# The order in which eight PSUM places are dealt out in the last part of a transformer-block kernel

## The chip, the cores and the metric

The kernel runs on one core of one Trainium2 chip. The metric is the device time of one execution in microseconds (us). Engines are named as in the profile: PE is TensorE's matmul (PEld its weight load), DVE is VectorE, ACT is ScalarE, POOL is GpSimd, SP is the engine whose queue issues most of the transfers.

## The reference

Four images ("b" from 0 to 3), 12 heads, 448 positions, 64 channels per head. The reference computes capped attention, then a channel MLP with a layer norm ahead of it, then a token mixer and a second channel MLP, all in float32:

```python
scores = cap * tanh(q @ k.T / sqrt(64) / cap); attn = softmax(scores); x = attn @ v   # (4, 448, 768)
xn = (x - mean) / sqrt(var + 1e-6) * g_ln
x = x + maximum(xn @ w_ch1, 0) @ w_ch2                   # 768 -> 3072 -> 768
u = x + (maximum(x.T @ w_tok1, 0) @ w_tok2).T            # 448 -> 256 -> 448
y = u + maximum(u @ u_ch1, 0) @ u_ch2                    # 768 -> 1536 -> 768
```

## The kernel before

All activations lie channel by position: six tiles of 128 channels by 448 positions for each image, `x2` and `x3` for the last two. To keep float32 accuracy every operand is split into a high and a low half in a reduced format, and a product of 128x128 weights with 128x448 activations is three matmuls (`PASSES`). A PSUM result is evacuated by DVE or ACT.

**The last part.** From line 914 on, images 2 and 3 go through both MLPs and the token mixer; that is the stretch from about 885 us to the end. It has these kinds of work, each with its own lines:

- Single image: `mlp` with one image (lines 920 and 925). Four hidden tiles, each 18 matmuls at L749 and evacuated by ACT at L754 and DVE at L755, then six output tiles of 12 matmuls at L770, each added into `x` by DVE at L774.
- Pair of images: `mlp` with images 2 and 3 (lines 921 and 926, five groups in all). Its hidden tiles come from `quads`: two quads per group, each a scheme of seven products (p1 to p7) of nine matmuls at L673, whose results are combined by DVE at L680 and ACT at L694 before the hidden tiles are made (L684, L685). Then six times two output tiles at L770, one for each image, added by DVE at L774. The operands of a quad are prepared by DVE, POOL and ACT (L609, L613, L173, L177).
- Token mixer: `tokens` (lines 922 and 923), transposes at L801, products at L825 and L847, evacuated at L804, L806, L833, L834, L851, woven with a single-image `mlp`.

**The places.** Every result takes the next place of a ring, by `next(main_banks)`. There are eight places of 512 float32 each: four one-bank tiles, `bank0` to `bank3`, and two tiles of two banks each, `sc0` and `sc1`, which attention uses whole and which the last part uses by halves:

```python
    BANKS = [Box(pp.tile([P, 512], F32, name=f"bank{i}")) for i in range(4)]
    sc_t = [pp.tile([P, 2, 512], F32, name=f"sc{i}") for i in range(2)]
    SCB = [Box(t[:, i]) for t in sc_t for i in range(2)]
```

So `SCB[0]` and `SCB[1]` are the halves of `sc0`, `SCB[2]` and `SCB[3]` those of `sc1`. In rows of the trace both halves of both tiles are called `sc`, and all four one-bank tiles `bank`.

**What sets the order.** The code does not run its steps as written: each is recorded with what it reads and writes, one `Box` for each half, and a planner (`Program.emit`) puts all steps into one order by its own fixed costs. Each engine runs its part of that order strictly in turn. The layer under the kernel then adds the waits between engines, from the tiles and the recorded order. Weights come through three tiles, `split0` to `split2`, each refilled by SP's queue (L341, L649) as soon as PE has used it.

Of the kernel before, what the change touches and what calls it, by code (L numbers as in the profile page):

```python
# [152 lines left out]
def block_kernel(ctx: ExitStack, tc: tile.TileContext, qkv, cap, gln, w1, w2, wt1, wt2, con, out):  # L153
# [72 lines left out]
# [3 lines that stand above are left out]
    SC = [Box(t, SCB[2 * i:2 * i + 2]) for i, t in enumerate(sc_t)]  # L229

    def ring(of):
        while True:
            yield from of
# [8 lines left out]
    def relay():  # L242

        def later(old, boxes, fill):
            old = [p for box in old for p in box.parts]
            add("place", 0, fill, (), old + boxes)

        def fill_x(b):
            t = place(f"late_x{b}", [3, 2, S], F32R, tag=f"x{b}")
            for i in range(3):  # L250
                LATE[b][i].at = t[:, i]

        for b in range(2):
            later(X[b], LATE[b], lambda b=b: fill_x(b))

        def fill_raw():
            for i in range(3):
                X3[i].at = place(f"late_raw{i}", [2, S], F32R, tag=f"raw{i}")
            X4[2].at = QS[0].at

        later(RAW + QS, [*X3, X4[2]], fill_raw)

        def fill_own():
            t = place("late_own", [2, 2, S], F32R, tag="own")
            for i in range(2):
                X4[i].at = t[:, i]

        later(own, X4[:2], fill_own)

        def fill_weights():  # L270
            for i in range(2):
                WF[i].at = place(f"late_whole{i}", [CC], tag=f"whole{i}")
            WF[2].at = place("late_pair", [CC], tag="pair_r")
            WF[3].at = v_t
            WS[0].at = halves_of(place("late_two", [2 * CC], F32R, tag="two"))
            WS[1].at = halves_of(place("late_qk", [2 * CC], F32R, tag="qk0"))
            WS[2].at = halves_of(ksvs_t[:, :2 * CC])

        later([*WHOLE, PAIR, *V, *two, *QK, *KS, *VS], [*WF, *WS], fill_weights)
        for box in (*EH, *EL):  # L280
            WS.append(Box(box.at[:, :, :CC], [box]))
# [3 lines left out]
    def setup():  # L285
        nc.scalar.dma_start(out=kc, in_=con[:, :K_PAIR])
        nc.scalar.dma_start(out=cap_t, in_=cap.to_broadcast([P, 1]))
        dve.memset(ones, 1.0)
        dve.memset(inv_c, 1.0 / C)
        (vs,) = VS  # L290
        dve.tensor_copy(vs.at[:, :, D:DV], ones.rearrange("p (c d) -> p c d", c=4))

        act(VA[0].at[:, 0], ones[:, :8], AF.Tanh)
        for t in rs_t:
            nc.gpsimd.memset(t, 0.0)
        dve.reciprocal(tsc, cap_t)
        dve.tensor_scalar_mul(tsc, tsc, 1.0 / math.sqrt(D))
        (sq,) = SQ
        prog.key = 15.0
        add("dma", 8, lambda: nc.scalar.dma_start(out=gl, in_=gln), (), [GL])  # L300
        add("dma", 3 * P, lambda: nc.scalar.dma_start(out=sq.at[:, :3 * P], in_=con[:, K_PAIR:]), (), [sq])

        add("dve", 8, lambda: dve.tensor_scalar_mul(gl, gl, -1.0 / 8192.0), (), [GL])
        add("dve", 3 * P, lambda: dve.tensor_copy(pair_r, sq.at[:, :3 * P].rearrange("p (a b) -> p a b", a=3)), [sq], [PAIR])
# [274 lines left out]
    def normalise(b):  # L579
        rstd = RSTD[0]  # L580
        eng = LN_ENGINES[b]
        for e in range(NCC):
            o, g = centred[e] if b < 2 else two[e % 2], BIG[b % 2][e]
            if b >= 2:
                subtract(b, e, o)
            add("dve+", S, lambda o=o, e=e: dve.scalar_tensor_tensor(
                o.at, o.at, gl[:, e:e + 1], rstd.at, op0=ALU.mult, op1=ALU.mult), [rstd, GL], [o])
            add("act", S, lambda g=g, o=o: act(g.at[:, 0], o.at, AF.Copy), [o], [g])  # L588
            add(eng, S, lambda eng, g=g, o=o: low(engine_of[eng], g.at[:, 1], o.at, g.at[:, 0]), [o], [g])
# [5 lines left out]
    main_banks = ring(BANKS)  # L595
# [19 lines left out]
    def sides(later):  # L615

        t0 = prog.key
        for c in range(3):
            prog.key = t0 + later + c * SIDES_PACE
            f12, f22, f11, f21 = (next(tmps) for _ in range(4))  # L620
            for to, pair in ((f11, BIG[0][c]), (f12, BIG[1][c]), (f22, BIG[1][c + 3]), (f21, BIG[0][c + 3])):
                join(to, pair, S)
            both(f11, f12, f11, ALU.subtract, S)
            split(X1[c], f11, S)
            both(f12, f22, f12, ALU.subtract, S)
            split(X3[c], f12, S)
            both(f22, f22, f11, ALU.subtract, S)
            split(X2[c], f22, S)
            both(f21, f21, f22, ALU.subtract, S)
            split(X4[c], f21, S)  # L630
        prog.key = t0
# [86 lines left out]
    def prepare(g):  # L718

        nonlocal n_tile  # L720
        rows = [(w1, g * G + i, C) for i in range(G)] + [(w2, g * NCC + e, G * P) for e in range(NCC)]
        for w, row, cols in rows:
            load(n_tile, w, row, cols)
            n_tile += 1
            prog.key += AHEAD_PACE
# [136 lines left out]
    def weave(*gens, ahead=0.0):  # L862

        gens, t0 = list(gens), prog.key
        keys = [t0 - ahead * (i == 0) for i in range(len(gens))]
        left = list(range(len(gens)))
        while left:
            for i in list(left):
                prog.key = keys[i]
                if next(gens[i], left) is left:  # L870
                    left.remove(i)
                keys[i] = prog.key
        prog.key = t0 + sum(k - t0 for k in keys) + ahead


    def groups(bs, first, n):
        return [(first + g, bs) for g in range(n)]

    with tc.manual_schedule():
        setup()  # L880
        prog.key = T_AHEAD
        ahead = True
        for g in range(N_AHEAD):
            prepare(g)
        ahead = False
        prog.key = 0.0
        attention(0, 0.0, 3.97)
        prog.key += T_LN0
        layer_norm(0)
        normalise(0)  # L890
        head_banks = side_banks = ring(BANKS[:2])
        attention(1, 60.01, 6.39)
        prog.key += T_LN1
        layer_norm(1)
        normalise(1)
        head_banks = side_banks = ring(BANKS[:1])

        main_banks = ring(BANKS[2:])
        n0, n1, n2 = N0, N1, N2
        prog.key, stretch = T_ALONE, STRETCH0  # L900
        weave(mlp(groups((0,), 0, n0)))
        main_banks = chain(BANKS[2:], ring(BANKS[1:]))
        attention(2, T_ATT2, PACE2)
        layer_norm(2)
        attention(3, T_ATT3, PACE3)
        prog.key, stretch = T_PAIR, STRETCH1
        weave(mlp(groups((0, 1), n0, NG1 - n0)))
        weave(tokens(0, HIDDEN[2]), mlp(groups((1,), 0, n0)), ahead=TOKENS_AHEAD)
        weave(tokens(1, HIDDEN[2]), mlp(groups((0,), NG1, N20)), ahead=TOKENS_AHEAD)
        weave(mlp(groups((0, 1), NG1 + N20, NG2 - N20), (0,)))  # L910
        weave(mlp(groups((1,), NG1, N20), (1,)))
        normalise(2)
        stretch = 1.0
        weave(mlp(groups((2,), 0, n1)))
        layer_norm(3)
        normalise(3)
        main_banks = ring(SCB + BANKS)
        relay()
        sides(SIDES_LATER)
        weave(mlp(groups((3,), 0, N30)))  # L920
        weave(mlp(groups((2, 3), n1, NG1 - n1)))
        weave(tokens(2, HIDDEN[2]), mlp(groups((3,), N30, n1 - N30)), ahead=TOKENS_AHEAD)
        weave(tokens(3, HIDDEN[2]), mlp(groups((2,), NG1, n2)), ahead=TOKENS_AHEAD)
        sides(SIDES_LATER)
        weave(mlp(groups((3,), NG1, n2)))
        weave(mlp(groups((2, 3), NG1 + n2, NG2 - n2), (2, 3)))
        prog.emit()
# [41 lines left out]
```

## Time and profile before

| | |
|---|---|
| time, median of 3 runs | 1380.13 us (1379.91 to 1381.29) |
| time of the profiled execution | 1379.54 us |
| its span, first to last instruction | 1377.7 us |
| PE busy | 1339.9 us, 97% |
| DVE busy | 1031.8 us, 75% |
| ACT busy | 658.5 us, 48% |
| mean granted TensorE clock | 0.996 of full speed |
| chain that ended last: PE | 90% of the span |

The profiled execution took 1.8 us more than its span, time that lies before the first and after the last instruction. A busy share says only that an engine was at work; what a change is worth is read from what PE waits for, as PE makes up 90% of the chain that ended last.

### The profile page before, as it was taken

What the parts mean: (1) busy time and instruction counts of PE and PEld (TensorE: products, weight loads), DVE (VectorE), ACT (ScalarE), POOL (GpSimd) and SP (SyncE); (2) the same over time, 40 slices, a digit from 0 to 9 for tenths busy, and PEclk for the clock granted to TensorE, in tenths of its full rate; (3) what the DMA queues carried; (4) which work ended last, traced back from release to release, by engine and by line L of the source; (5) the groups of instructions that cost most, each with busy time, mean ns of one, the idle gap of its engine ahead of it and who ended that gap; (6) DMA issues with size and microseconds to landing.
All of it is one profiled execution on the core that took longest, in us unless ns stands there. A gap on an engine that the chain in (4) does not pass through costs nothing.

```text
span 1377.7 us, 17881 instructions
## 1 busy us (share of the span) xinstructions
PE 1339.9 (97%) x6378; PEld 1154.8 (84%) x6378; DVE 1031.8 (75%) x1819; ACT 658.5 (48%) x1081; POOL 161.2 (12%) x133
## 2 busy tenths in 40 slices
PE   8999999999999999999999999989999999999998
PEld 3334679999999999999999999878888889888887
DVE  5988699999999998999988787857456332358572
ACT  8996566666756656667663563212112111212120
POOL 2420000100101001001101020221202000013020
PEclk9999999999999999999999999999999999999999
DMA  8885447757575765577565666653324345445233
GB/s 275 282 271 163 128 149 238 253 191 246 188 264 178 247 226 156 197 230 240 190 231 196 214 214 206 205 186 106 130 84 127 103 137 169 153 153 176 91 109 126
DMA packets 131865, 255.88 MB, mean 186 GB/s; under 512 B 9920, under 2 KB 70592, under 8 KB 131776
## 3 DMA queue, kind: packets, MB, share of 16 engines
q1 hardware_dynamic: 131200, 254.45, 56.8%
q8 instruction: 50, 0.82, 0.2%
q10 hardware_dynamic: 576, 0.29, 0.1%
q14 instruction: 39, 0.32, 0.1%
HBM read 192.57 MB, written 62.13 MB: 185 GB/s over the span
## 4 chain that ended last, share of the span: by engine, by line
PE 90%; DVE 4%; ACT 4%; DMA 1%; issue 1%; ACTq 0%; DVEq 0%
PE bank L770 30%; PE bank L749 25%; PE sc L770 8%; PE bank L673 5%; PE sc L673 5%; PE sc L749 3%; PE sc L411 3%; PE bank L429 3%; PE bank L453 2%; PE bank L825 2%; PE bank L847 1%; ACT x L414 1%; PE sc L408 1%; ACT x L415 1%; DVE x L774 1%; DVE m L419 1%
## 5 line engine op out<-in xcount | busy, mean ns | idle before, releaser
L770 PE MATMUL bank<-h,split 128*128 128x448 f32 x2064 | 437.7, 367 | 1.4 <-DVE x L774 1.3
L770 PEld LDWEIGHTS bank<-h,split 128*128 128x128 f32 x2064 | 386.1, 188 | 34.9 <-DVE x L774 2.1
L749 PE MATMUL bank<-big,split 128*128 128x448 f32 x1656 | 354.2, 368 | 3.5 <-ACT big L588 1.8
L749 PEld LDWEIGHTS bank<-big,split 128*128 128x128 f32 x1656 | 310.5, 188 | 33.4 <-ACT big L588 2.9
L774 DVE TENSOR_TENSOR x<-x,bank 128x448 f32<-128x448 f32 x172 | 105.9, 617 | 82.9 <-PE bank L770 81.7
L770 PE MATMUL sc<-h,split 128*128 128x448 f32 x528 | 115.2, 369 | 10.0 <-DVE x L774 9.3
L770 PEld LDWEIGHTS sc<-h,split 128*128 128x128 f32 x528 | 97.7, 188 | 22.9 <-DVE x L774 14.1
L173 POOL TENSOR_TENSOR ksvs<-qk,ksvs 64x512 fp32r<-64x512 f32 x23 | 32.1, 1397 | 644.1 <-ACT ksvs L392 625.0
L321 ACT ACTIVATE whole<-raw 128x384 f32<-128x384 f32 (+2 forms) x130 | 77.6, 601 | 40.7 <-DVE split L173 36.9
L754 ACT ACTIVATE h<-bank 128x448 fp32r<-128x448 f32 x92 | 49.9, 542 | 89.9 <-PE bank L749 89.5
L324 DVE SCALAR_TENSOR_TENSOR whole<-raw,whole 128x384 int32<-128x384 int32 (+2 forms) x130 | 84.2, 650 | 0.2
L774 DVE TENSOR_TENSOR x<-x,sc 128x448 f32<-128x448 f32 x44 | 27.0, 620 | 72.7 <-PE sc L770 70.8
L177 ACT ACTIVATE split<-whole 128x384 fp32r<-128x384 f32 (+1 forms) x96 | 54.2, 567 | 54.3 <-PE bank L770 33.3
L322 ACT ACTIVATE raw<-raw 128x384 int32<-128x384 uint32 (+2 forms) x130 | 77.5, 600 | 0.0
L755 DVE SCALAR_TENSOR_TENSOR h<-bank,h 128x448 fp32r<-128x448 f32 x92 | 56.6, 616 | 26.6 <-ACT h L754 25.6
L325 DVE CUSTOM_DVE_ANT_0 whole<-raw,whole 128x768 uint16<-128x768 uint16 (+2 forms) x116 | 74.2, 642 | 0.0
L173 DVE TENSOR_TENSOR split<-whole,split 128x384 fp32r<-128x384 f32 (+1 forms) x112 | 69.2, 621 | 3.7 <-ACT split L177 3.3
L419 DVE TRANSPOSE_TENSOR_REDUCE m<-x 128x28 f32<-128x896 f32 x48 | 52.7, 1103 | 10.5 <-ACT x L415 10.0
L177 ACT ACTIVATE late_two<-v 128x384 fp32r<-128x384 f32 x10 | 5.3, 526 | 113.1 <-DVE v L613 113.1
L323 DVE TENSOR_SCALAR whole<-whole 128x384 int32<-128x384 int32 (+2 forms) x130 | 55.0, 426 | 3.6 <-ACT whole L321 3.2
L419 DVE TRANSPOSE_TENSOR_REDUCE m<-own 128x28 f32<-128x896 f32 x48 | 52.9, 1101 | 4.9 <-ACT own L415 4.9
L414 ACT ACTIVATE own<-sc,tsc 128x896 f32<-128x896 f32 x48 | 47.9, 1001 | 11.6 <-DVE el L173 6.1
(295 smaller groups left out, 1997.9 us busy)
## 6 DMA issues: line engine op xcount, KB each, us to landing
split<-kept SPq DMA_DIRECT2D x96, 512.0 KB, 3.7
split<-kept SPq DMA_DIRECT2D x118, 384.0 KB, 4.1
raw<-in_w SPq DMA_DIRECT2D x72, 384.0 KB, 3.7
kept<-split SPq DMA_DIRECT2D x72, 384.0 KB, 3.5
raw<-in_w SPq DMA_DIRECT2D x54, 512.0 KB, 4.3
kept<-split SPq DMA_DIRECT2D x54, 512.0 KB, 3.3
qk<-in_qkv SPq DMA_DIRECT2D x34, 480.0 KB, 3.7
v<-in_qkv SPq DMA_DIRECT2D x31, 192.0 KB, 3.2
```

Of the source, the lines that this page charges most:

```text
L173: eng.tensor_tensor(out, whole, high.bitcast(F32), op=ALU.subtract)
L177: act(out, a, AF.Copy)
L321: add("act", m, lambda: act(f.bitcast(F32), hi.bitcast(F32), AF.Copy, scale=2.0 ** -112), [r], [w])
L322: add("act", m, lambda: act(lo, lo.bitcast(U32), AF.Copy, scale=2.0 ** -29), (), [r])
L324: add("dve+", m, lambda: dve.scalar_tensor_tensor(f, hi, -(1 << 31), f, op0=ALU.bitwise_and, op1=ALU.bitwise_or), [r], [w])
L325: add("pool+" if ahead else "dve+", m, lambda e: engine_of[e].tensor_tensor(f, f, lo, op=ALU.add), [r], [w])
L414: add("act", 2 * S, lambda e=e, sc=sc: act(e, sc.at[:, :, :S], AF.Tanh, scale=tsc), [sc], eb)
L419: add("dve", 2 * S, lambda half=half, e=e: dve.tensor_reduce(m.at[:, half].rearrange("p c j -> p (c j)"), e.rearrange("p c (j i) -> p (c j ...
L673: mm(bank.at[:, :S], w.at[:, wi, c * P:(c + 1) * P], x[c].at[:, xi], start=(c, n) == (0, 0), stop=(c, n) == (2, 2))
L749: mm(ph.at[:, :S], w[:, wi, cc * P:(cc + 1) * P], src[cc].at[:, xi], start=(cc, n) == (0, 0), stop=(cc, n) == (NCC - 1, 2))
L770: mm(py.at[:, :S], w[:, wi, i * P:(i + 1) * P], h[i].at[:, hi], start=(i, n) == (0, 0), stop=(i, n) == (G - 1, 2))
L774: add("dve", S, lambda x=x, py=py: dve.tensor_tensor(x.at, x.at, py.at[:, :S], op=ALU.add), [py], [x], early=EVACUATE)
```

## The change

One line: the order of the ring that the last part draws its places from.

```diff
-        main_banks = ring(SCB + BANKS)
+        main_banks = ring([SCB[0], BANKS[0], SCB[2], BANKS[1], SCB[1], BANKS[2], SCB[3], BANKS[3]])
```

The ring still has the same eight places, and each still comes round after eight results. Before, the order was `sc0` first half, `sc0` second half, `sc1` first, `sc1` second, `bank0` to `bank3`. After it, the first and second half of `sc0` are four results apart, as are those of `sc1`, with one-bank tiles between them. The sequence of instructions on every engine, apart from the names of these places, is the same in both programs, on PE, DVE, ACT, POOL and SP.

On PE, near the end of the program, in the output tiles of the last pair group (L770; `h` are hidden tiles, `split` weights), the difference reads:

```order
 L770 MATMUL sc0_117<-h4_90,split1_78 128x448 x3
 L770 MATMUL sc0_117<-h5_91,split1_78 128x448 x3
-L770 MATMUL sc0_117<-h3_89,split1_78 128x448 x3
-L770 MATMUL sc0_117<-h2_88,split1_78 128x448 x3
-L770 MATMUL sc0_117<-h7_93,split1_78 128x448 x3
-L770 MATMUL sc0_117<-h6_92,split1_78 128x448 x3
+L770 MATMUL bank0_113<-h3_89,split1_78 128x448 x3
+L770 MATMUL bank0_113<-h2_88,split1_78 128x448 x3
+L770 MATMUL bank0_113<-h7_93,split1_78 128x448 x3
+L770 MATMUL bank0_113<-h6_92,split1_78 128x448 x3
 L770 MATMUL sc1_118<-h0_86,split2_79 128x448 x3
```

The output tile of image 3 that followed image 2's in the other half of `sc0` now lies in `bank0`.

On PE, in the second quad of the last pair group (L673), seven products and what they lie in; before:

```order
L673 MATMUL bank0_113<-big1_85,ksvs_102 128x448 x9
L673 MATMUL bank1_114<-big0_84,split1_78 128x448 x9
L673 MATMUL bank2_115<-big0_84,split1_78 128x448 x9
L673 MATMUL bank3_116<-late_x0_5958,late_two_6983 128x448 x9
L673 MATMUL sc0_117<-late_x1_6262,late_qk_6984 128x448 x9
L673 MATMUL sc0_117<-late_raw0_6504,eh0_103 128x448 x3
L673 MATMUL sc0_117<-late_raw1_6505,eh0_103 128x448 x3
L673 MATMUL sc0_117<-late_raw2_6506,eh0_103 128x448 x3
L673 MATMUL sc1_118<-late_own_6638,el0_104 128x448 x6
```

and now:

```order
L673 MATMUL sc0_117<-big1_85,ksvs_102 128x448 x9
L673 MATMUL bank2_115<-big0_84,split1_78 128x448 x9
L673 MATMUL sc1_118<-big0_84,split1_78 128x448 x9
L673 MATMUL bank3_116<-late_x0_5958,late_two_6983 128x448 x9
L673 MATMUL sc0_117<-late_x1_6262,late_qk_6984 128x448 x9
L673 MATMUL bank0_113<-late_raw0_6504,eh0_103 128x448 x3
L673 MATMUL bank0_113<-late_raw1_6505,eh0_103 128x448 x3
L673 MATMUL bank0_113<-late_raw2_6506,eh0_103 128x448 x3
L673 MATMUL sc1_118<-late_own_6638,el0_104 128x448 x6
```

Of the two products with `big0` the second moved from `bank2` to a half of `sc1`; the products with `ksvs` and `late_x1` now lie in the two halves of `sc0`, and the one with `late_raw` between them and `late_own` has left `sc0` for `bank0`. Products in the two halves of one tile stand apart, with others between them, where before the halves of `sc0` were written one right after the other.

On DVE, at the same place, the reads of those products (L680) and the hidden tiles made from them (L685); before:

```order
L680 TENSOR_TENSOR rstd0_112<-sc1_118,mean0_111 128x448
L680 TENSOR_TENSOR other0_100<-sc1_118,other0_100 128x448
L680 TENSOR_TENSOR mean0_111<-bank0_113,mean0_111 128x448
L680 TENSOR_TENSOR other0_100<-sc1_118,other0_100 128x448
L685 SCALAR_TENSOR_TENSOR h0_86<-sum0_99,h0_86 128x448
L685 SCALAR_TENSOR_TENSOR h2_88<-rstd0_112,h2_88 128x448
L685 SCALAR_TENSOR_TENSOR h1_87<-other0_100,h1_87 128x448
L685 SCALAR_TENSOR_TENSOR h3_89<-mean0_111,h3_89 128x448
L680 TENSOR_TENSOR sq0_98<-sc0_117,rsm_108 128x448
L680 TENSOR_TENSOR rsm_108<-bank2_115,rsm_108 128x448
```

and now:

```order
L680 TENSOR_TENSOR rstd0_112<-sc1_118,mean0_111 128x448
L680 TENSOR_TENSOR other0_100<-sc1_118,other0_100 128x448
L680 TENSOR_TENSOR mean0_111<-sc0_117,mean0_111 128x448
L680 TENSOR_TENSOR other0_100<-bank1_114,other0_100 128x448
L685 SCALAR_TENSOR_TENSOR h0_86<-sum0_99,h0_86 128x448
L685 SCALAR_TENSOR_TENSOR h2_88<-rstd0_112,h2_88 128x448
L685 SCALAR_TENSOR_TENSOR h1_87<-other0_100,h1_87 128x448
L685 SCALAR_TENSOR_TENSOR h3_89<-mean0_111,h3_89 128x448
L680 TENSOR_TENSOR sq0_98<-sc0_117,rsm_108 128x448
L680 TENSOR_TENSOR rsm_108<-sc1_118,rsm_108 128x448
```

The reads `mean` and `rsm` moved from one-bank tiles into halves of `sc0` and `sc1`, whose other halves PE writes close by.

## Rows read from the trace of the kernel before

**Rows 1.** Who PE waited for: us in total, times, longest us.

```profile
PE sc L770 <- DVE x L774: 9.3, 13, 0.7
PE sc L749 <- DVE h L755: 2.1, 2, 1.4
PE sc L801 <- DVE x L774: 1.8, 3, 0.7
PE sc L749 <- ACT h L754: 1.3, 2, 0.7
PE sc L749 <- DVE h L834: 0.7, 1, 0.7
PE sc L770 <- DVE x L851: 0.7, 1, 0.7
PE sc L749 <- ACT h L833: 0.3, 1, 0.3
PE bank L770 <- DMA split<-kept: 0.2, 1, 0.2
```

**Rows 2.** Timeline, output tiles of the fourth pair group: start, us, engine, line, operation, count.

```profile
1300.65 3.81 PE L770 MATMUL sc<-h,split 128*128 128x448 f32 x18
1300.85 0.62 DVE L774 TENSOR_TENSOR x<-x,bank 128x448 f32<-128x448 f32 x1 [1.81 <-PE bank L770]
1304.50 0.62 DVE L774 TENSOR_TENSOR x<-x,sc 128x448 f32<-128x448 f32 x1 [3.03 <-PE sc L770]
1305.18 5.12 PE L770 MATMUL sc<-h,split 128*128 128x448 f32 x24 [0.71 <-DVE x L774]
...
1311.01 1.48 PE L770 MATMUL sc<-h,split 128*128 128x448 f32 x6 [0.71 <-DVE x L774]
```

**Rows 3.** Timeline, output tiles of the fifth pair group.

```profile
1342.73 9.89 PE L770 MATMUL bank<-h,split 128*128 128x448 f32 x48
```

**Rows 4.** Timeline, second quad of the fifth pair group.

```profile
1329.97 3.81 PE L673 MATMUL bank<-big,split 128*128 128x448 f32 x18
1332.43 0.62 DVE L680 TENSOR_TENSOR rstd<-sc,mean 128x448 f32<-128x448 f32 x1
1333.50 0.61 DVE L680 TENSOR_TENSOR mean<-bank,mean 128x448 f32<-128x448 f32 x1
...
1335.44 1.99 PE L673 MATMUL sc<-late_x,late_qk 128*128 128x448 f32 x9
1336.17 0.62 DVE L685 SCALAR_TENSOR_TENSOR h<-mean,h 128x448 fp32r<-128x448 f32 x1
...
1339.09 1.38 PE L673 MATMUL sc<-late_own,el 128*128 128x448 f32 x6
1339.29 0.62 DVE L680 TENSOR_TENSOR sq<-sc,rsm 128x448 f32<-128x448 f32 x1 [2.50 <-PE sc L673]
1339.94 0.62 DVE L680 TENSOR_TENSOR rsm<-bank,rsm 128x448 f32<-128x448 f32 x1
```

**Rows 5.** Timeline, token mixer of image 3, transposes and first product.

```profile
1181.07 0.62 DVE L774 TENSOR_TENSOR x<-x,sc 128x448 f32<-128x448 f32 x1 [1.69 <-PE sc L801]
...
1181.12 1.30 PE L825 MATMUL bank<-big,t 128*128 128x384 f32 x6
1181.72 0.49 ACT L804 ACTIVATE big<-sc 128x384 fp32r<-128x384 f32 x1 [2.93 <-DVE x L774]
```

**Rows 6.** Timeline, token mixer of image 3, a later product.

```profile
1210.86 1.05 PE L825 MATMUL bank<-h,t 128*128 128x384 f32 x5
1211.06 0.62 DVE L774 TENSOR_TENSOR x<-x,sc 128x448 f32<-128x448 f32 x1
```

**Rows 7.** One weight load by its line, window 1247.7 to 1248, and its user.

```profile
L341 SPq DMA_DIRECT2D split<-kept x1: 518/518/518, 1247.8 to 1247.8; - x1
...
DMA to landing us min/median/max: 3.7/3.7/3.7
1252.14 2.70 PE L770 MATMUL sc<-h,split 128*128 128x448 f32 x12 [0.71 <-DVE x L774]
```

## The prediction

> **What bounds the kernel now.** I read first whom PE waited for, since PE makes up 90% of the chain that ended last. From 850 us on it waited 23 times for DVE or ACT, always ahead of a matmul into `sc`, 16.2 us in all: 9.3 + 2.1 + 1.8 + 1.3 + 0.7 + 0.7 + 0.3; ahead of a matmul into `bank` only 0.2 us, and that for a load [rows 1]. Both kinds of place hold the same sort of results, so the wait belongs to the two-bank tiles.
>
> The timeline of a pair group's output tiles shows how it comes about. The 18 matmuls that start at 1300.65 are the 12 of image 2 in the first half of `sc0` and the first 6 of image 3 in the second half. The read of the first half (`x<-x,sc`) starts at 1304.50, when all 18 are done (1300.65 + 3.81 = 1304.46), although its own 12 had ended 1.2 us before (6 x 0.2); the read of a `bank` place starts at 1300.85, while PE is already 0.2 us into the next place. And PE's next matmul, the seventh into the second half, starts at 1305.18, that is 0.06 us after the read of the first half ends at 1304.50 + 0.62, with 0.71 us idle [rows 2]. So reads and writes of the two halves wait for each other as if the tile were one place: the read for those writes to the other half that stand ahead of it in the recorded order, then the writes behind it for the read.
>
> **What the Trainium skill says of it.** Its page "PSUM — Partial Sum Buffer", section "PSUM bank collisions raise a hardware error", tells to guard PSUM by bank and quadrant, and calls each bank a separate RAM; by that rule two halves that are two banks need no wait on each other. The trace shows them waiting all the same [rows 2], so the wait is the program's and not the chip's. If the program guarded by banks, as the page has it, these stalls would have another cause and the sum would be 0 in place of what follows.
>
> **What a stall costs.** More than its idle time. Without stalls matmuls of this shape start 0.2027 us apart: 48 take 9.89 [rows 3] and 18 take 3.81 [rows 2], so 30 more take 6.08. From 1305.18 to 1311.01 there are 24 matmuls and one stall: 5.83 us, where 24 x 0.2027 = 4.865 would do. A stall of 0.71 idle thus costs 0.965, or 0.255 above the idle time, which is what PE loses of overlap between one matmul and the next. For 23 stalls: 16.2 + 23 x 0.255 = 22.1 us. That is all that can be won: the span without them is 22.1 shorter, if nothing else is late.
>
> **What the change removes.** In the output tiles of the pair groups, in the single-image stages and in the mixer the two halves no longer stand next to each other, and by the waits that the instructions of the changed program carry, followed each to the instruction that raises it, none of the 23 is left. All 22.1 us are counted as won there. The reads in question even start 1.2 us sooner after their products, which hides nothing else, as DVE waits for PE around them [rows 2].
>
> **What it adds.** The same coupling now acts at other places, between results four apart in the ring, where a place is held long.
>
> *Quads.* Six DVE reads (L680) now wait for a product in the other half, all six in the quads. In the last group's second quad, `rstd<-sc` ran at 1332.43; now it waits for the second of the two `big` products, which ends at 1329.97 + 3.81 = 1333.78, so it starts at about 1333.82, 1.39 us late. The reads behind it follow late by the same: `mean` (1333.50 + 0.61) ends at 1335.50 and not at 1334.11. It now lies in `sc0`, and the PE product at 1335.44 goes into the other half of `sc0`; 0.06 after the read is 1335.56, 0.12 late. The last of the hidden tiles then ends at 1336.17 + 0.62 + 1.39 = 1338.18. Next, `sq<-sc` does not have to wait for the neighbouring product any more (it had 2.50 idle before 1339.29) and can start at 1338.1; `rsm`, which starts 0.65 behind it, ends at 1338.1 + 0.65 + 0.62 = 1339.37, so PE's product at 1339.09, moved to 1339.21 by the first wait, can start at 1339.43: another 0.22 [rows 4]. Together 0.34, and some 0.1 for lost overlap: 0.45. The same pattern stands in the second quads of the second and third groups: 3 x 0.45 = 1.35. Bounds: nothing if the reads lie a little better; and if `rsm` kept its present end (1339.94 + 0.62 = 1340.56) the product at 1339.09 would wait 1.5 and cost with overlap 1.65, three times 4.95. I take 1.35, as the read's own wait ahead of it is gone. The other three late reads are late by no more than this one, and what PE next writes into those tiles comes later; I take nothing, with 3 x 1.65 as the upper bound.
>
> *Mixer.* At 1181.12 the product at L825 now lies in the second half of `sc1`, and ACT reads transposes out of the first half. ACT ran that read at 1181.72 because it waited for a DVE add on the other half; without that it can start when that add did, 1181.07, when the transposes were done, and ends at 1181.07 + 0.49 = 1181.56. PE starts at 1181.62, 0.5 late [rows 5]; with 0.1 of overlap 0.6. At 1210.86 the product at L825 now waits for the DVE add out of the other half, which ends at 1211.06 + 0.62 = 1211.68: 1211.74, late by 0.88 [rows 6], with overlap 0.98. Together 1.6. Nothing hides these two.
>
> *Loads.* Where a stall vanishes PE comes for its weights sooner. The load issued at 1247.8 lands 3.7 later at 1251.5, and its user at 1252.14 stood in a stall [rows 7]; a stalled matmul starts 0.88 late (1305.18 - 1300.65 - 18 x 0.2027 [rows 2]), so it would have come at 1251.26, and now waits until about 1251.55: 0.29, with overlap 0.4. One more load, at the entry of the first quads, stands about as tight, and I price it the same, an estimate: 0.7 together, bounds 0 and the two whole stalls that they cover, 1.9.
>
> **The sum.** 22.1 - (1.35 + 1.6 + 0.7 = 3.65) = 18.45 us. The profiled execution took 1379.54, so 1361.1. That execution was 0.6 below the median of the runs; on the median's footing 1361.7, and I write 1361.4.
>
> **The rivals.**
>
> *More is given back.* If the six late reads each cost PE the upper bound, 6 x 1.65 = 9.9 in place of 1.35, with mixer and loads as above: 22.1 - 9.9 - 2.3 = 9.9, or 1369.6; half of that, 1365. For it: the margins that PE has behind late reads are tenths of a us (0.12 and 0.22 above). Against: the read that matters most had 2.50 us of idle time ahead of it, which the change frees [rows 4].
>
> *Loads become the bound.* In the single-image stages load follows load, and 7 of the 23 stalls lie there. If loads left all of them worth nothing, 7 x 0.97 = 6.8 goes, and the time is 1361.4 + 6.8 - 0.7 = 1367.5. For it: the margin of 0.65 between landing and user at 1252.14. Against: that load was issued as its tile came free, so most loads move with PE.
>
> *No change.* The stalls are not of halves but of reads that come late in any place; then they move along to `bank` and the time is 1380. That is how it would be by the rule by banks of the Trainium skill's page "PSUM — Partial Sum Buffer". Against it stand 0.2 us ahead of `bank` and 16.2 ahead of `sc` [rows 1], and the read that starts 1.2 us after its own product's end [rows 2].
>
> *Slower.* One mechanism, in the quads: a read waits for a nine-matmul product in the other half (1.99 us long), and PE's next product into that tile waits for the read, up to 1.99 + 0.62 + 0.06, some 2.7 with overlap. The 22.1 won are used up from 9 such stalls on. The five groups have ten quads, so it would have to come about in nearly each; the changed program has six reads that wait, and in three of them PE comes close behind. With 14 it would be 1380 - 22 + 38 = 1396.
>
> **How the numbers follow.** Two results of this kernel differ from no change when they are 0.2% apart, 2.8 us (the three runs span 0.1%). The forecast has 0.70: its own range runs from 1358.5 (the added 3.65 nearly nothing) to 1364 (the quads cost twice, the loads 1.9). More given back has 0.15, loads 0.08, no change 0.04, slower 0.03. Lower than 1357.4 (1379.5 - 22.1) nothing reaches, unless stalls cost more than I found. I let the range go from 1358 to 1368, which takes in loads and most of the larger give-back, and leaves out about 0.15. Faster by over 0.2%: 0.70 + 0.15 + 0.08 = 0.93; within: 0.04; slower: 0.03.
>
> **What would show it.** Right: in the list of PE's waits the row `sc L770 <- DVE x L774` falls from 9.3 us to nearly nothing, the reads of `sc` start about 0.05 us after their own product, 48 matmuls in a row at L770 with no idle time wherever a pair group's outputs are made. PE's busy time stays about 1340 while the span falls by 18. The added waits show as short ones ahead of L673 for DVE L680 (at most three groups), and two ahead of L825. Wrong: waits of 1 us and more at L673, waits for loads ahead of L749 or L770, or waits ahead of `bank` in place of those ahead of `sc`.

## The result, and the profile after

The changed kernel takes 1363.6 us, median of 4 runs (1362.26 to 1367.25); beside it on the same chip the kernel before took 1380.02. The ratio is 0.989, 95% interval 0.986 to 0.992: faster by 16.4 us. A second set of four runs gave 1363.65 and 0.989 (0.987 to 0.990). The profiled execution of after is the slowest of its four, 1367.25 us, with a span of 1365.5.

Its list of PE's waits from 850 us on (us in total, times, longest us), which answers [rows 1]:

```profile
PE sc L825 <- DVE x L774: 0.8, 1, 0.8
PE bank L770 <- DMA split<-kept: 0.5, 2, 0.3
PE sc L825 <- ACT big L804: 0.3, 1, 0.3
```

The seven rows ahead of `sc`, 23 waits and 16.2 us, are gone. Two short ones in the mixer are new, and nothing has moved to `bank` but 0.3 us more for loads.

Timeline of after, the output tiles that [rows 2] showed:

```profile
1288.77 2.59 PE L770 MATMUL bank<-h,split 128*128 128x448 f32 x12
1288.97 0.62 DVE L774 TENSOR_TENSOR x<-x,sc 128x448 f32<-128x448 f32 x1 [1.81 <-PE sc L770]
1291.20 2.60 PE L770 MATMUL sc<-h,split 128*128 128x448 f32 x12
1291.40 0.62 DVE L774 TENSOR_TENSOR x<-x,bank 128x448 f32<-128x448 f32 x1 [1.81 <-PE bank L770]
1293.63 2.59 PE L770 MATMUL bank<-h,split 128*128 128x448 f32 x12
```

Each read of `sc` now starts 0.20 after PE has begun the next place, as each read of `bank` does, and PE goes on from place to place without idle time: 12 matmuls every 2.43 us, 12 x 0.2027.

Timeline of after, the quad of [rows 4]:

```profile
1320.39 1.99 PE L673 MATMUL sc<-big,split 128*128 128x448 f32 x9
1322.21 1.99 PE L673 MATMUL bank<-late_x,late_two 128*128 128x448 f32 x9
1322.41 0.62 DVE L680 TENSOR_TENSOR rstd<-sc,mean 128x448 f32<-128x448 f32 x1 [1.42 <-PE sc L673]
...
1323.48 0.61 DVE L680 TENSOR_TENSOR mean<-sc,mean 128x448 f32<-128x448 f32 x1
...
1324.24 2.06 PE L673 MATMUL sc<-late_x,late_qk 128*128 128x448 f32 x9
...
1326.14 1.99 PE L673 MATMUL bank<-late_raw,eh 128*128 128x448 f32 x9
...
1327.33 0.62 DVE L680 TENSOR_TENSOR rsm<-sc,rsm 128x448 f32<-128x448 f32 x1
...
1328.01 1.51 PE L673 MATMUL sc<-late_own,el 128*128 128x448 f32 x6
...
1329.36 0.78 PE L673 MATMUL sc<-qs,el 128*128 128x448 f32 x3
```

`rstd` waits for the product in the other half (1320.39 + 1.99 = 1322.38); `mean` ends at 1324.09 and PE follows at 1324.24; `rsm` ends at 1327.95 and PE follows 0.06 later. Nine matmuls take 1.824 undisturbed, but from 1322.21 to 1324.24 there are 2.03 and on to 1326.14 there are 1.90: 0.28 late. From 1326.14 to 1328.01 it is 1.87, and the six behind, 1.24 at this stretch's 0.2067, take 1.35: 0.16 more. Together 0.44. The list of waits shows none of it, since hardly any idle time is left between the modelled ends of the matmuls. It is seen only in the distances between starts. The view names nobody ahead of the start at 1324.24, 0.15 after `mean` ended; that the tile is the cause there rests on e1 below, where the same matmuls follow each other without a delay.

The two products in the mixer, after:

```profile
1173.79 1.31 PE L825 MATMUL sc<-big,t 128*128 128x384 f32 x6 [0.25 <-ACT big L804]
...
1204.34 1.11 PE L825 MATMUL sc<-h,t 128*128 128x384 f32 x5 [0.80 <-DVE x L774]
```

Not all of the difference of the spans, 12.2 us, is the change's. The same matmul, behind the same wait for a load, starts in the kernel before, after, and in a second execution of after (e2 below) at

```profile
886.54 1.65 PE L770 MATMUL bank<-h,split 128*128 128x448 f32 x7 [0.17 <-DMA split<-kept]
...
890.78 1.47 PE L770 MATMUL bank<-h,split 128*128 128x448 f32 x6 [0.23 <-DMA split<-kept]
...
887.15 1.66 PE L770 MATMUL bank<-h,split 128*128 128x448 f32 x7 [0.30 <-DMA split<-kept]
```

Up to here the programs are the same, and the profiled execution of after had lost 4.24 us of its own. One piece of it is a lower granted clock from 120 to 130 us, 0.83 by the row of after (columns: busy us of PE, PEld, DVE, ACT, POOL, then granted clock, DMA share, GB/s), where the other two have 1.00; 0.83 is a mean over the two levels:

```profile
120.00:130.00 10.00, 8.28 (x31) 5.09 (x31) 9.97 (x20) 6.82 (x11) 0.00 (x0) 0.83 0.34 99
```

So I compare the last part alone: from this matmul to the start of the last one, 487.1 us before and 470.6 after, 16.5 won (470.3 and 16.9 in e2).

**Where the last part's time goes, in all kernels.** For each matmul I took the smallest distance to the next one's start that any of seven traces with the same matmuls shows; these sum to 462.5 us. What a trace has above this sum is of two kinds. One is rhythm: undisturbed matmuls of 448 columns follow each other either quickly, in distances that go round between 199 and 207 ns and are 202.7 ns on average, or slowly, 206 or 207 ns every time. The other is interruptions: waits, with the overlap that they cost. A delay that all the traces have is in the 462.5 and not above it. The last column but one counts the matmuls in the slow rhythm, 0.2067 us apart and not 0.2027; where a series begins and ends can be drawn a little differently, by some ten matmuls to a trace.

| kernel | time, median | ratio (95%) | last part | interruptions | slow matmuls | rhythm |
|---|---|---|---|---|---|---|
| before | 1380.0 | | 487.1 | 23.0 | 416 | 1.6 |
| after | 1363.6 | 0.989 (0.986 to 0.992) | 470.6 | 3.8 | 1069 | 4.3 |
| e2, after again | 1363.65 | 0.989 (0.987 to 0.990) | 470.3 | 5.0 | 694 | 2.8 |
| e1, four tiles | 1361.1 | 0.987 (0.985 to 0.989) | 468.4 | 1.5 | 1086 | 4.3 |
| e8, e1 again | 1359.5 | 0.985 (0.983 to 0.987) | 465.6 | 1.5 | 388 | 1.5 |
| e3, one pair apart | 1370.6 | 0.994 (0.992 to 0.995) | 477.5 | 13.0 | 488 | 1.9 |
| e4, `bank` first | 1383.7 | 1.003 (1.002 to 1.005) | 491.1 | 26.1 | 624 | 2.5 |
| e7, two apart | 1369.8 | 0.994 (0.992 to 0.996) | 481.1 | 12.4 | 1544 | 6.2 |
| e6, six places | 1364.6 | 0.990 (0.988 to 0.992) | 470.4 | | 447 | 1.8 |
| e5, four tiles + transpositions | 1358.1 | 0.986 (0.984 to 0.988) | 466.6 | 3.3 | 193 | 0.8 |
| e9, e5 again | 1360.0 | 0.987 (0.985 to 0.989) | 465.6 | 2.9 | 33 | 0.1 |
| e10, after + transpositions | 1360.3 | 0.986 (0.984 to 0.988) | 469.7 | 6.0 | 273 | 1.1 |

(e6's matmuls stand in another order from a point on, so its interruptions are not worked out; in e5, e9 and e10 that column holds the 16 added transpositions too.)

### The profile page after: what moved, and what is told of

It is laid out like the page before. It is cut to its first block, busy times and chain, and to the rows that moved or that the text cites. A ratio compares the mean times of both kernels' runs of the same rounds, so it can differ in the third digit from the quotient of the medians.

```text
span 1365.5 us, 17912 instructions
## 1 busy us (share of the span) xinstructions
PE 1343.7 (98%) x6378; PEld 1156.7 (85%) x6378; DVE 1032.4 (76%) x1819; ACT 658.5 (48%) x1081; POOL 161.5 (12%) x133
## 4 chain that ended last, share of the span: by engine, by line
PE 91%; ACT 4%; DVE 3%; DMA 1%; issue 1%; ACTq 0%
PE bank L770 31%; PE bank L749 27%; PE sc L770 7%; PE sc L673 5%; PE bank L673 5%; PE sc L411 3%; PE bank L429 3%; PE bank L453 3%; PE bank L825 2%; PE bank L847 1%; ACT x L414 1%; PE sc L408 1%; PE sc L749 1%; ACT x L415 1%; DVE m L419 1%; PE sc L847 1%
## 5 line engine op out<-in xcount | busy, mean ns | idle before, releaser
L770 PE MATMUL bank<-h,split 128*128 128x448 f32 x2088 | 449.4, 367 | 1.8 <-DVE x L774 1.3
L770 PEld LDWEIGHTS bank<-h,split 128*128 128x128 f32 x2088 | 390.1, 188 | 37.4 <-DVE x L774 1.8
L749 PE MATMUL bank<-big,split 128*128 128x448 f32 x1800 | 387.0, 369 | 3.5 <-ACT big L588 1.8
L749 PEld LDWEIGHTS bank<-big,split 128*128 128x128 f32 x1800 | 337.5, 189 | 37.0 <-ACT big L588 2.9
L754 ACT ACTIVATE h<-bank 128x448 fp32r<-128x448 f32 x100 | 54.3, 543 | 119.6 <-PE bank L749 119.2
L770 PE MATMUL sc<-h,split 128*128 128x448 f32 x504 | 111.8, 367 | 0.0
L770 PEld LDWEIGHTS sc<-h,split 128*128 128x128 f32 x504 | 94.4, 188 | 8.6 <-DVE rstd L613 0.3
L755 DVE SCALAR_TENSOR_TENSOR h<-bank,h 128x448 fp32r<-128x448 f32 x100 | 61.7, 617 | 44.5 <-ACT h L754 43.5
L774 DVE TENSOR_TENSOR x<-x,sc 128x448 f32<-128x448 f32 x42 | 26.1, 621 | 57.6 <-PE sc L770 57.3
L414 ACT ACTIVATE own<-sc,tsc 128x896 f32<-128x896 f32 x48 | 48.0, 1002 | 11.6 <-DVE el L173 6.1
```

Of the source, the lines that this page charges most:

```text
L414: add("act", 2 * S, lambda e=e, sc=sc: act(e, sc.at[:, :, :S], AF.Tanh, scale=tsc), [sc], eb)
L749: mm(ph.at[:, :S], w[:, wi, cc * P:(cc + 1) * P], src[cc].at[:, xi], start=(cc, n) == (0, 0), stop=(cc, n) == (NCC - 1, 2))
L755: add("dve", S, lambda ht=ht, ph=ph: dve.scalar_tensor_tensor(ht.at[:, 1], ph.at[:, :S], 0.0, ht.at[:, 0].bitcast(F32), op0=ALU.max, op1=A ...
L770: mm(py.at[:, :S], w[:, wi, i * P:(i + 1) * P], h[i].at[:, hi], start=(i, n) == (0, 0), stop=(i, n) == (G - 1, 2))
L774: add("dve", S, lambda x=x, py=py: dve.tensor_tensor(x.at, x.at, py.at[:, :S], op=ALU.add), [py], [x], early=EVACUATE)
```

## The experiments

The theory A is that of the prediction: reads and writes of the two halves wait for each other because they are one tile.

### e1: the old order, the halves as tiles of their own

When the last part begins, the two-bank tiles are given up and four one-bank tiles take their banks. The sequence of instructions on each engine stays.

```diff
+    halves = ExitStack()
+    sp = halves.enter_context(tc.tile_pool(name="sp", bufs=1, space=bass.MemoryType.PSUM))
...
-    sc_t = [pp.tile([P, 2, 512], F32, name=f"sc{i}") for i in range(2)]
+    sc_t = [sp.tile([P, 2, 512], F32, name=f"sc{i}") for i in range(2)]
...
-        main_banks = ring(SCB + BANKS)
+        FOUR = [Box() for _ in range(4)]
+        def fill_four():
+            halves.close()
+            hp = ctx.enter_context(tc.tile_pool(name="hp", bufs=1, space=bass.MemoryType.PSUM))
+            for i in range(4):
+                FOUR[i].at = hp.tile([P, 512], F32, name=f"sc{i}")
+        add("place", 0, fill_four, (), SCB + FOUR)
+        main_banks = ring(FOUR + BANKS)
```

> The order of the kernel before (halves next to each other), but from the last part on each half is a tile of its own, in the same four banks. Theory A (reads and writes of two halves wait for each other because they are one tile): all 23 stalls ahead of the former halves are gone although the order is the old one, and the late reads of the quads and the two waits of the mixer that the changed order brought do not come either. The changed kernel loses 1.2 us in its quads and 1.35 in its mixer, so this kernel ends at 1363.6 - 2.5 = about 1361, between 1358 and 1364. Theory B (the stalls come from two neighbouring banks that are written and read one after the other, on the chip itself): the order is the old one, the stalls stay and the time is 1378 to 1381.

1361.1 us. PE's waits from 886 us on:

```profile
PE bank L675 <- DMA split<-kept: 0.6, 1, 0.6
PE bank L772 <- DMA split<-kept: 0.3, 1, 0.3
```

Not one wait for DVE or ACT is left, in the order that had 23. Theory B falls: the same banks are written and read one after the other as before. (In the built program the four tiles are banks 4 to 7, in the order in which the halves of `sc0` and `sc1` lay in them.) This also agrees with what the Trainium skill's page "PSUM — Partial Sum Buffer", section "PSUM bank collisions raise a hardware error", says of each bank being a separate RAM; the wait between halves was the tile's. Interruptions are 1.5 against 3.8 in after: the give-back of quads and mixer is gone too.

### e3: one pair apart, the other together

```diff
-        main_banks = ring(SCB + BANKS)
+        main_banks = ring([SCB[0], SCB[1], BANKS[0], SCB[2], BANKS[1], BANKS[2], SCB[3], BANKS[3]])
```

> Only the halves of sc1 are dealt out apart, those of sc0 stay next to each other. Theory A: about half of the stalls stay, 11 in place of 23, 9 of them of 0.7 us at the output tiles and at the transposes, and at some 0.9 us each the time lies 10 us above the changed kernel: 1371 to 1375. A rival C (the time was won by something else in the new order, the stalls being only where PE's slack shows): the time is that of the one or of the other, within 3 us of 1363.6 or of 1380.

1370.6 us, 0.4 below the range that A gave (1371 to 1375), and between the two kernels, which rival C had excluded. PE's waits, the first four rows:

```profile
PE sc L770 <- DVE x L774: 5.0, 7, 0.7
PE sc L749 <- DVE h L755: 1.4, 1, 1.4
PE sc L801 <- DVE x L774: 1.1, 2, 0.7
PE sc L749 <- DVE h L834: 0.7, 1, 0.7
```

In all 13 waits for DVE or ACT, 9.2 us, where 11 were expected. Its interruptions are 10.0 below those of before, which has 10 such waits more, and 11.5 above those of e1, which has 13 fewer: 1.0 and 0.9 us for each wait.

### e4: the halves still together, other results in them

```diff
-        main_banks = ring(SCB + BANKS)
+        main_banks = ring(BANKS + SCB)
```

> The ring begins with the four one-bank tiles; the halves stay next to each other, but other results fall into them. Theory A: the stalls move and are not fewer: some 21, about 16 of them ahead of L770 and L801 and, new, three in the quads ahead of L673, so that the time is again 1376 to 1384. A rival D (certain results, in their place in the program, come late and would stall in any tile): the stalls stay where they were, ahead of the same results (the seventh matmul after image 2's output tile at 1305.18 and 1311.01 of the kernel before), now partly in bank.

1383.7 us. Three of its eleven rows of waits for DVE or ACT, with 25 waits and 18.3 us:

```profile
PE sc L770 <- DVE x L774: 9.3, 13, 0.7
PE sc L673 <- DVE sum L680: 1.6, 2, 0.8
...
PE sc L673 <- DVE mean L680: 0.8, 1, 0.8
```

All are ahead of `sc` and none ahead of `bank`. The stalls went with the places, to other results, three of them in the quads as expected. Rival D falls.

### e6: six places, no two of them in one tile

```diff
-        main_banks = ring(SCB + BANKS)
+        main_banks = ring([SCB[0], SCB[2], *BANKS])
```

> A ring of six places: the four one-bank tiles and the first half of each two-bank tile; the second halves stay unused. No two places are parts of one tile. Theory A: what costs is the coupling of halves and not the number of places: two or three stalls, where a place comes round after six results, at 0.9 us and 0.25 us of overlap each, and no other give-back: 1362 to 1366, near the changed kernel and 14 us or more under the kernel before although it has two places fewer. Rival E (PE waits because places come round too soon): with a quarter of the places gone more than ten stalls, and 1370 or more.

1364.6 us: two places fewer than before, and 15 us faster. The waits for DVE or ACT:

```profile
PE sc L673 <- ACT ksvs L177: 0.7, 1, 0.7
PE bank L825 <- DVE x L774: 0.7, 1, 0.7
PE sc L673 <- DVE x L774: 0.7, 1, 0.7
PE bank L673 <- DVE x L774: 0.7, 1, 0.7
PE bank L673 <- DVE sq L680: 0.2, 1, 0.2
```

The first is for an operand of the product, `ksvs`; four are for places, three of 0.7 us and a short one, where A had two or three. Rival E, more than ten stalls and 1370 or more, falls. The comparison is not as clean as the others: with six places the planner puts the steps in another order on PE, DVE, ACT and POOL.

### e7: the halves two places apart

```diff
-        main_banks = ring(SCB + BANKS)
+        main_banks = ring([SCB[0], SCB[2], SCB[1], SCB[3], *BANKS])
```

> The ring takes both first halves and then both second halves, so that the halves of a tile come two places apart and not four. Theory A: what counts is which reads and writes fall close to each other: none of the 23 stalls stays, but five others come, three of them in the single-image stages and the mixer, together 4.0 us idle and 5.3 with overlap, where the changed kernel gives back 2.55 in quads and mixer: 1363.6 + 2.7 = about 1366, between 1364 and 1369. Rival F (any distance above one is as good as four): the time of the changed kernel, 1362 to 1364, with its two waits in the mixer or none.

1369.8 us: rival F falls, but my own figure was too low as well. There are 9 waits for DVE or ACT, 7.5 us, where I had counted 5 and 4.0:

```profile
PE sc L749 <- DVE h L755: 2.1, 2, 1.3
PE sc L770 <- DVE rsm L680: 1.2, 1, 1.2
PE sc L801 <- DVE h L755: 1.2, 1, 1.2
```

My count took each read to follow right behind its product; at L755 DVE reads the place only behind ACT's L754, and this longer chain, 3.3 us in three waits, I had left out. The rest of the miss is rhythm: 6.2 us against 4.3 in after.

### e2: the changed kernel once more

> The changed kernel once more, as the neighbour of the others on one chip. Theory A and B alike: 1363.6, between 1361 and 1367. Its profile shows what repeats from one execution to the next: if the two rhythms of the matmuls of 448 columns (one every 0.2027 us or one every 0.2067 us) are set by the program, the stretch from 921 to 1002 us has 0.2067 again; if each interruption of PE draws them anew, the stretches in either rhythm lie elsewhere, and the span differs by up to 3 us for that alone.

1363.65 us. The same program, in the stretch where after ran slowly, the window from 930 to 995 us, first after and then e2:

```profile
930.00:995.00 65.00, 65.00 (x316) 59.04 (x315) 42.63 (x66) 13.08 (x25) 14.63 (x12) 1.00 0.38 121
...
930.00:995.00 65.00, 65.00 (x322) 60.23 (x322) 42.03 (x65) 12.84 (x26) 13.05 (x11) 1.00 0.35 114
```

PE is busy throughout and the granted clock is 1.00 in both, yet e2 gets six matmuls more through. In after all 394 matmuls from 921 to 1002 us are 0.2067 apart, in e2 the 349 from 927 to 998 us 0.2027. So the program does not set it. With PE quicker there, loads are reached sooner, which fits that e2 waits 1.5 us for three loads and after 0.5 for two.

### e5, e8, e9, e10: small transpositions ahead of the matmuls

In the first six traces (before, after, e1 to e4) the matmuls behind L831, a transposition of 128 columns that the kernel already does at one place per image, are quick, and those that come right behind a product group at L825 (384 columns) are in the slow rhythm in all 44 series of five or more. So I added 16 such transpositions, six behind other groups of L825 and ten ahead of a quad's first product, to the program of e1 (e5, e9) and to the changed kernel (e10):

```diff
             def product():
+                if reset:
+                    nc.tensor.transpose(bank.at[:, :P], ident, ident)
                 for c in range(3):
...
-            p1 = times(a11, b11)
+            p1 = times(a11, b11, True)
...
+                        if part == 1 and b >= 2 and not (last and j == 1):
+                            nc.tensor.transpose(pj.at[:, CC:CC + P], ident, ident)
```

> Four one-bank tiles in place of the two-bank tiles, as before, and 16 small transpositions more: one of 128 columns after each product group of the mixer that has none yet, into columns that the result leaves free, and one ahead of the first product of each quad, into its place, which that product then overwrites. Theory R (each interruption of PE draws the rhythm of the matmuls of 448 columns anew, 0.2027 or 0.2067 us, and a small transposition nearly always draws the quick one, as behind L831 in every trace): of the 1086 matmuls in the slow rhythm behind 886 us fewer than 350 are left, 3.0 us won at 4.0 ns each; 16 transpositions at 0.11 us (26 + 286 ns in place of 203) cost 1.8, and loads that PE now reaches sooner take up to 1: 1359.5 to 1362. Rival N (the rhythm comes from what else runs, transfers above all): the slow matmuls stay about 1000, and the time is 1.8 us above that of the four tiles, about 1363.

1358.1 us, below the 1359.5 to 1362 expected, and 193 slow matmuls in place of 1086. The start of the output tiles behind a group of L825 in e1 (there L827), and the same with the transposition in e5 (there L829 and L832):

```profile
1127.60 1.03 PE L827 MATMUL bank<-h,t 128*128 128x384 f32 x5
1128.47 2.64 PE L772 MATMUL bank<-h,split 128*128 128x448 f32 x12
1130.94 2.23 PE L772 MATMUL sc<-h,split 128*128 128x448 f32 x10
...
1124.55 1.03 PE L829 MATMUL bank<-h,t 128*128 128x384 f32 x5
1125.42 0.27 PE L832 MATMUL bank<-kc 128*128 128x128 f32 x1
1125.44 2.67 PE L774 MATMUL bank<-h,split 128*128 128x448 f32 x12
1127.96 2.40 PE L774 MATMUL sc<-h,split 128*128 128x448 f32 x11
```

In e1 a series of 90 matmuls 0.2067 apart begins; in e5 the 89 behind are 0.2027 apart, after 0.09 us more at the first (1127.96 - 1125.44 = 2.52 against 2.43). So it is at each place: in e5, e9 and e10 all 48 series that follow such a single transposition of `ident` directly are quick, and all 10 of five or more that still follow a product group directly are slow. Rival N falls.

Not every transposition of 128 columns does this. The mixer's groups of three at L801, which transpose `x`, are followed by slow series too: in 6 cases of 10 in the kernel before, the longest 46 matmuls from 1199.6 us on, and in 15 of the 61 series of six or more in the first six traces. In the three traces with the added ones none of 33 is slow. What makes the difference is not shown.

Whether it pays was the question of the next three, run side by side:

> The four one-bank tiles once more, beside the next two. Theory R and rival N alike: 1361, between 1359 and 1364; half or more of the matmuls of 448 columns behind 886 us may run in the slow rhythm or only a quarter, as it is drawn.

> Four one-bank tiles with the 16 small transpositions once more. Theory R: behind 886 us again fewer than 350 matmuls in the slow rhythm, and the time 1 to 3 us below that of the four tiles without them: 1358 to 1360. Rival G (the first gap of 3.0 us between the two was the chance of two different sets of runs): no difference, or 1.8 us more for the added transpositions.

> The changed kernel, with its new order of places and its two-bank tiles, and the same 16 transpositions. Theory R: its slow matmuls behind 886 us fall from 694 to 1069 to fewer than 350, worth 1.5 to 3 us, less 1.8 for the transpositions and up to 1 for loads; the waits of its quads still come and may draw the slow rhythm for the rest of a group: 1361 to 1364. Rival N (the rhythm does not depend on what stands ahead): 1365.4, that is 1.8 above 1363.6.

e8 took 1359.5, e9 1360.0, e10 1360.3, which is below the 1361 to 1364 expected. In the profile the count of theory R, fewer than 350, holds each time: 33 slow matmuls in e9, 273 in e10. But e8, the program of e1, had only 388 by itself this time. The same 48 matmuls in e1 and in e8:

```profile
960.41 10.08 PE L772 MATMUL bank<-h,split 128*128 128x448 f32 x48
...
961.95 9.89 PE L772 MATMUL bank<-h,split 128*128 128x448 f32 x48
```

Against a lucky e8 the 16 transpositions win nothing: 465.6 us of last part in both. Rival G holds for the time: that the transpositions pay on the average is not shown. e10 is 3.4 us below the changed kernel, with intervals of the ratios that overlap.

**The best version.** The four one-bank tiles: 1360.2 us, median of the eight runs of e1 and e8 (1355.9 to 1364.0), against 1363.7 for the eight of the changed kernel (1361.1 to 1367.3). The intervals of the ratios still overlap a little. With the transpositions the nine runs of e5 and e9 have 1359.4, which is no clear difference.

## Why the prediction was right, and where it was off

1363.6 measured, 1361.4 predicted. By its own steps:

- *The stalls are the two-bank tiles' own and cost more than their idle time.* Right: e1 takes away the tiles and keeps the order, e4 keeps the tiles together and moves the results. Of the 23.0 us of interruptions in the kernel before, the 23 stalls taken one by one make up 22.0; 22.1 was the term.
- *Quads, 1.35.* Measured 1.2, in the same three groups and at the same two products of each (0.41, 0.38 and 0.44). `rsm` moved forward as worked out. That the added waits would show as short ones ahead of L673 was wrong in form: they show in no list of waits.
- *Mixer, 1.6.* From a few matmuls ahead of each of the two products to a few behind it, after takes 0.50 and 0.93 us more than before: 1.4. Both came where they were put, with idle times of 0.25 and 0.80 for the 0.5 and 0.88 expected; with the lost overlap they cost 0.50 and 0.93 for 0.6 and 0.98, so both were a little over-sized.
- *Loads, 0.7.* About 0.6 in after and 1.7 in e2 by the smallest distances. These leave out the load that was named, since all the traces lose as much there or more: its user, at 1252.14 in the kernel before, comes at 1243.27 in after and 1239.52 in e2, 0.23 and 0.25 late, where 0.4 was the price. With it 0.9 and 1.95: in the one execution near the term, in the other at its upper bound of 1.9. The second load, at the entry of the first quads, costs nothing in after and 0.9 in e2. The rival that loads take 6.8 is not borne out, nor is the one that the late reads give back 5 to 10.
- *No change, slower.* Both fell with the list of waits.

The interruptions thus fell by 19.2 us (18.0 in e2), where the sum had 18.45. What failed is the step *without stalls matmuls of this shape start 0.2027 us apart*: they start 0.2027 or 0.2067 apart, and the sum has no term for that. (*PE's busy time stays about 1340* can't be judged from one execution: 1343.7 in that of after, 1338.3 in e2.) With the stalls gone more matmuls ran 0.2067 apart: 653 more than before in after and 278 more in e2, at 4.0 ns each 2.6 and 1.1 us. 19.2 - 2.6 = 16.6 and 18.0 - 1.1 = 16.9: the 16.5 and 16.9 that the last part won, and near the 16.4 of the medians. How many matmuls are slow differs between executions of the same program (1086 in e1, 388 in e8), so it is in part luck that the time came no further than 2.2 us from the forecast.

The yardstick of 0.2% was too narrow: the 17 runs of the kernel before that were taken beside e1 to e4 span 1375.6 to 1384.2, 0.6%. The change of 1.1%, with an interval from 0.8 to 1.4, is clear of it all the same.

Whether stalls keep PE in the quick rhythm is likely but not settled. Of the series of ten matmuls or more right behind a distance of over 0.9 us all 16 in the profile of before are quick, and 37 of 42 in the first six traces. Without stalls a series in the slow rhythm lasts longer: up to 394 matmuls in after and 722 in e1. But e7, with nine waits, has the most slow matmuls of all, and one execution to a program is too few for an average.

## What to carry to other kernels

Two places that are halves of one tile are one place for the waits: don't deal them out one after the other, or better make each place a tile of its own. Fewer places that are free of each other did better here than more that are coupled. Measure a wait by the distance between starts and not by the idle time alone: here each of the 23 stalls cost PE a quarter of a microsecond more (22.0 against 16.2 us idle), and a short one shows hardly any idle time (in the quads of after six of them, 1.2 us in all, are in no list of waits).

## What the runs showed of the hardware that was not expected

Matmuls of 128x128 by 128x448 run back to back in one of two rhythms, 0.2027 or 0.2067 us from start to start, at a granted clock of 1.00 in both. A series nearly always keeps its rhythm until the next interruption, for up to 722 matmuls (149 us); in e1 and e4 one turned quick at 892 us, and in e6 and e7 one turned slow, with no distance above 0.21 us there. Right behind a single transposition of `ident`, 128 columns, all 66 series of the twelve traces were quick, and 33 to 273 slow matmuls were left of some 2100 in the three traces with the added ones; right behind a product group of 384 columns all 44 series of five or more in the first six traces were slow, and behind the groups of three transpositions at L801 15 of 61. The same program differs by 698 slow matmuls, 2.8 us, between two executions (e1 and e8). What decides it inside TensorE stays open.
